# Gates split into parts already in the first batch, and p ahead of the next d in units 20 and 40

## The chip, the cores and the metric

The kernel runs on one core of a Trainium2 chip. The metric is the time of one execution on the device in microseconds (us). Before the change the median of three runs is 284.43 us.

## The reference

Two blocks follow one another. First an attention with sketched features: for each of 4 batches and 4 heads, with 1088 positions and head dimension 32,

```python
def phi(x):
    a = np.einsum('rd,bhsd->bhsr', S1, x)
    b = np.einsum('rd,bhsd->bhsr', S2, x)
    return np.einsum('bhsi,bhsj->bhsij', a, b).reshape(*x.shape[:-1], r * r)
q_p, k_p = (phi(q), phi(k))
kv = np.einsum('bhsf,bhsd->bhfd', k_p, v)
z = np.sum(k_p, axis=2)
num = np.einsum('bhsf,bhfd->bhsd', q_p, kv)
den = np.einsum('bhsf,bhf->bhs', q_p, z)[..., None] + 1e-06
attn = num / den
```

with r = 8. Its output becomes x, 4352 tokens by 128 channels. Then a gated feed-forward block with 1536 hidden channels: `g = x @ w_gate`, `val = x @ w_val`, `out = (g * sigmoid(g) * val) @ w_out`. The inputs q, k and v are float32; the sketches and weights come as float64 and are narrowed in the kernel.

## The kernel before, in words

The tokens stand on the free axis: `xT` holds x transposed, 128 channels by 4352 tokens. The hidden channels are 12 chunks of 128. A **unit** is one chunk for one block of tokens: a gate product and a value product on TensorE into PSUM, a Silu on ScalarE (`sg`), and their product on VectorE, written to a slot of `hbuf` or `late`. A **down product** multiplies such a slot by a chunk of `wo` and adds to the output block's PSUM bank; after 12 of them the block is turned and stored.

The instructions are put down in one order that is written out by hand, and each engine works through its own part of it. There are two stages.

*First batch* (tokens 0 to 1087, blocks 0 to 2 of 384, 384 and 320 tokens). `unit` (L1020) makes plain FP32 products. Six of its units are "late" ones: ScalarE copies the value product out, and GpSimd multiplies it by `sg` afterwards (`catch_up`, L1047); `doubles` (L964) finds room for these six `sg`. The other thirty units of the batch are emitted by the loop over `z`, 0 to 29; from z = 17 on each is followed by a down product and by a piece of the next batch's attention (`parts_of(1)`, which advances the generator `attentions`). The loop also splits the value weights `wv` (see below). After it, a `while todo` loop emits the remaining down products three at a time with the rest of the attention of batch 1: the denominators and products of query features (`query_step`, L744, tiles `dot`, `den`, `phq`, `phT`) on VectorE, and at last `numerators` (L773), 64 small matmuls (L783) that are copied to `xT` (L800) half by ScalarE and half by VectorE.

*Later blocks* (`line`: blocks 3 to 9, six of 480 tokens and one of 384; 84 units numbered y = 0 to 83). Here products are split. A weight w is parted by `cut_weights` (L841) in four rows of steps: w1 = a shortened copy (ScalarE), low = w - w1 (VectorE for `wg`, GpSimd for `wv`), wb = low x 4096 (ScalarE), and wd = w1 - wb (one operation on VectorE or GpSimd). All are recorded as L872. Tokens are split likewise by `cut_tokens` (L874) into x1, x0 and xd. A split product is three passes in the faster FP32R type, added in PSUM: **d** is wd by xd (L985, in `start_unit`), which ScalarE then scales in place in PSUM (L989); **p** is w1 by x1 and wb by x0 (L1004 and L1005, in `finish_unit`), added on top of the scaled d. Silu (L1007) and the product (L1012) follow.

`start_unit(y + 1)` is emitted ahead of `finish_unit(y)`, so that the scaling of one unit lies beside the passes of the one before. A unit takes a pair of PSUM banks from `pair()`, which chooses among three pairs the one used longest ago. Down products come after `finish_unit(y)`, once more than five hidden chunks are waiting; in units 0 to 4 there is none. At y in `GROUPS` (4, 6, 20, 22, 40) a group of small matmuls of the attention of the coming batches is put in front; at 20 and 40 it begins with `numerators`, which takes two pairs.

In units 0 to 19 only the value product is split: the gate product is a plain FP32 matmul (L999). The weights of the gates are split during units 0 to about 10, with `low` in `late`. From y = 20 (`GATES`) on both are split. The tile names show it: `w`, `wb`, `wd` are the parts of `wv`, and `graw`, `gphq` those of `wg`. Some chunks of blocks 6 to 8 have split down products, too; they aren't touched.

Of the kernel before, what the change touches and what calls it, by code (L numbers as in the profile page):

```python
# [7 lines left out]
FP32 = mybir.dt.float32  # L8
# [4 lines left out]
AF = mybir.ActivationFunctionType  # L13
# [6 lines left out]
def kernel(  # L20
# [28 lines left out]
    nc = tc.nc  # L49
    P = nc.NUM_PARTITIONS  # L50
# [18 lines left out]
    BW = 64 * XS  # L69
# [33 lines left out]
    def hold(*tags):  # L103
        for t in tags:
            held.update((place[t], place[t] + 1) if t in "ab" else (place[t],))
# [761 lines left out]
    def take(steps, n):  # L867

        for _ in range(n):
            if steps:  # L870
                f, args = steps.pop(0)
                f(**args)  # L872
# [86 lines left out]
            out=hd, in0=whole(h0), scalar=-BETA, in1=whole(h1), op0=ALU.mult, op1=ALU.add  # L959
        ))  # L960

    room = [None, 2]

    def doubles(k):  # L964

        if room[1] + k > 2:
            room[:] = fpool.tile([P, 2, WB], FP32, tag="sgl", name="sum", bufs=4), 0
        at = room[1]
        room[1] += k
        return room[0][:, at : at + k, :]  # L970

    WHOLE = 1.0 + 1.0 / BETA
    sums_of = {}

    def start_unit(y, both=False):

        i, j = line[y // NCH], y % NCH
        n = blocks[i][1]  # L980
        xd = x_parts[i][2][:, 0:n]
        ws = (wg, wv) if both else (wv,)
        ps = sums_of[y] = pair(y)[:, :, 0:n]
        for w in ws:
            nc.tensor.matmul(  # L985
                ps[:, w is wv], w_parts[id(w), j // 3][2][:, j % 3, :], xd, start=True, stop=True
            )
        d = ps if both else ps[:, 1]
        nc.scalar.activation(d, d, AF.Copy, scale=-1.0 / BETA / WHOLE)  # L989

    def finish_unit(y, both=False):
        i, j = line[y // NCH], y % NCH
        t0, n = blocks[i]
        x1, x0, _ = (x[:, 0:n] for x in x_parts[i])
        ps = sums_of.pop(y)
        now(before, y)
        for w in (wg, wv):
            if w is wg and not both:
                nc.tensor.matmul(  # L999
                    ps[:, 0], wg[:, j, :], xT[:, t0 : t0 + n], start=True, stop=True  # L1000
                )
                continue
            w1, wb = (w_parts[id(w), j // 3][k][:, j % 3, :] for k in range(2))
            nc.tensor.matmul(ps[:, w is wv], w1, x1, start=False, stop=False, skip_group_check=True)  # L1004
            nc.tensor.matmul(ps[:, w is wv], wb, x0, start=False, stop=True, skip_group_check=True)  # L1005
        sg = fpool.tile([P, WB], FP32, tag="sg", name="sg", bufs=5)[:, 0:n]
        nc.scalar.activation(sg, ps[:, 0], AF.Silu, scale=WHOLE if both else 1.0)  # L1007
        slot_of[i, j] = slots.pop(0)
        hj = slot_of[i, j]
        hidden[i, j] = hj  # L1010
        todo.append((i, j))
        nc.vector.scalar_tensor_tensor(  # L1012
            out=hj[:, 0:n], in0=ps[:, 1], scalar=WHOLE, in1=sg, op0=ALU.mult, op1=ALU.mult
        )
        let_go(y)
        now(behind, y)
        if (i, j) in DOWN:
            cut_hidden(y, i, j)

    def unit(i, j, late=False, between=(None, None)):  # L1020


        t0, n = blocks[i]
        g, u = bank(), bank()
        for o, w in ((g, wg), (u, wv)):
            if between[0] and w is wv:
                between[0]()
            nc.tensor.matmul(  # L1028
                o[:, 0:n], w[:, j, :], xT[:, t0 : t0 + n], start=True, stop=True
            )  # L1030
        sg = doubles(1)[:, 0, :] if late else fpool.tile([P, WB], FP32, tag="sg", name="sg", bufs=5)
        nc.scalar.activation(sg[:, 0:n], g[:, 0:n], AF.Silu)  # L1032
        slot_of[i, j] = slots.pop(0)
        hj = slot_of[i, j]
        hidden[i, j] = hj
        todo.append((i, j))
        if late:
            if between[1]:
                between[1]()
            nc.scalar.copy(hj[:, 0:n], u[:, 0:n])  # L1040
            lates.append((hj[:, 0:n], sg[:, 0:n]))
        else:
            nc.vector.tensor_tensor(  # L1043
                out=hj[:, 0:n], in0=sg[:, 0:n], in1=u[:, 0:n], op=ALU.mult
            )

    def catch_up():  # L1047
        o, sg = lates.pop(0)
        nc.gpsimd.tensor_tensor(out=o, in0=o, in1=sg, op=ALU.mult)


    def down(y=None):

        i, j = todo.pop(0)
        n = SPLIT if i == LAST else blocks[i][1]
        if j == 0:
            acc[i] = bank("g1" if i == 1 else "g2" if i in line[2::2] else "acc")
        mine = [c for c in range(NCH) if (i, c) in DOWN]
        if mine and j == mine[0]:
            acc[i, "p"] = bank("acc" if i in line[2::2] else "g2")  # L1060
        sides = dict(start=(j == 0), stop=(j == NCH - 1))
        if j in mine:
            w1, wb, wd = [down_parts[x][:, FINE.index(j), :] for x in ("w1", "wb", "wd")]
            h1, h0, hd = h_parts.pop((i, j))
            nc.tensor.matmul(acc[i][:, 0:n], wd, hd, **sides)  # L1065
            p = acc[i, "p"][:, 0:n]
            nc.tensor.matmul(p, w1, h1, start=(j == mine[0]), stop=False)  # L1067
            nc.tensor.matmul(p, wb, h0, start=False, stop=(j == mine[-1]))  # L1068
            if j == mine[-1]:
                copy_out(y, i, n)  # L1070
        else:
            w = down_parts["scaled"][:, PLAIN.index(j), :] if mine else wo[:, j, :]
            nc.tensor.matmul(acc[i][:, 0:n], w, hidden[i, j][:, 0:n], **sides)  # L1073
        if i != LAST:
            hidden.pop((i, j))
            slots.append(slot_of[i, j])
        if j == NCH - 1:
            if mine:
                put_together(y, i, n)
            else:  # L1080
                store(i, n)
# [209 lines left out]
    for z, (i, j) in enumerate(seq):  # L1291
        if z == 17:
            free_banks.pop()
            turn[0] %= 4
        unit(i, j)
        for p in parts.get(z, ()):
            part(*p)
        if z in (24, 25, 26):
            catch_up()
        if z == 6:  # L1300
            load_k(1)
            load_v(1, [nc.sync] * 4)
            load_q(1)
        if z >= 17:
            todo.remove(order[0])
            todo.insert(0, order.pop(0))
            down()
        if z == 20:
            lows = [
                pool.tile([P, 3, P], FP32, tag=tag, name="low", bufs=bufs)[:]  # L1310
                for pool, tag, bufs in ((apool, "qb", 2), (apool, "dT", 2), (apool, "rd", 2), (apool, "qb", 2))
            ]
            first, low, second, third = cut_weights(wv, lows, nc.gpsimd)
        if z in (20, 21):
            take(first, 2)
        if z == 21:
            take(low, 3)
        if z == 25:
            take(second, 3)
        if z >= 17:  # L1320
            parts_of(1)
        if z == 26:
            take(low, 1)
            take(third, 3)
        if z == 29:
            take(second, 1)
            take(third, 1)
    todo.sort()
    x_steps = None
    while todo:  # L1330
        for _ in range(min(3, len(todo))):
            down()
        if begun[0] and not x_steps:
            x_steps = cut_tokens(HEAD, nc.vector)
            run(x_steps)
        parts_of(1 + (begun[0] and len(todo) > 2))
# [7 lines left out]


    END = len(line) * NCH
    GROUPS, GATES = (4, 6, 20, 22, 40), 20

    token_steps = {}
    for m, i in enumerate(line[1:], 1):  # L1350
# [2 lines left out]
            token_steps.setdefault(at, []).append(gen)  # L1353
    oldest[0] = True
    hold("acc")
    lows = [late[:, c, :].rearrange("p (c f) -> p c f", f=P) for c in range(4)]
    gate_rows = []
    down_steps = cut_down()
    start_unit(0)
    for y in range(END):  # L1360
        if y in GROUPS:
            group()
        if y == GATES:
            hold("g2")
        if y + 1 < END:
            start_unit(y + 1, y + 1 >= GATES)
        finish_unit(y, y >= GATES)
        for _ in range(2):

            if len(todo) > min(5 + (todo[0] == (line[1], 0)), END - y + 1):  # L1370
                down(y)
        parts_of(y < GATES or y % 2 == 0)
        if y == 0:
            gate_rows = cut_weights(wg, lows, nc.vector)
        for n, row in enumerate(gate_rows):
            if y >= (0, 2, 6, 6)[n]:
                take(row, 1)
        for gen in token_steps.get(y, ()):
            next(gen, None)
        if y in range(24, 38, 2):  # L1380
            next(down_steps, None)
# [43 lines left out]
```

## Time and profile before

| | us |
|---|---|
| median of 3 runs | 284.43 (284.11 to 284.86) |
| the profiled execution's own time | 284.74 |
| its span, first to last instruction | 283.0 |
| TensorE busy | 275.2 |
| ScalarE busy | 175.2 |
| VectorE busy | 174.1 |
| GpSimd busy | 75.3 |

The profile is of one execution. PE is TensorE, DVE VectorE, ACT ScalarE, POOL GpSimd; L12 is line 12 of the kernel. A row of the timeline gives the start, the busy time, the engine, the line and the operation, the tile that is written and the one that is read, and how many instructions it holds; in brackets the idle time before it and what ended it. TensorE works on several matmuls at a time, so starts and durations of neighbouring rows overlap; the period from one row to the next of its kind is the measure. An FP32 matmul is recorded as two. The granted clock of TensorE was 0.997.

The first batch's last numerators are at about 87 us, unit 0 begins at 93 us, unit 20 lies near 142 us, unit 40 near 189 us.

### The profile page before, as it was taken

How to read it: one execution, taken by the hardware profiler on the slowest of the kernel's cores; microseconds unless marked ns; L12 is line 12 of the kernel's file. 1: busy time of each engine (PE TensorE's matmuls, PEld its weight loads, DVE VectorE, ACT ScalarE, POOL GpSimd, SP SyncE). 2: the span in 40 equal slices, each digit the busy share in tenths (PEclk: the TensorE clock that was granted, in tenths of full speed). 3: DMA queues.
4: the chain of work that ended last, by engine and by line, in shares of the span. 5: the costliest groups of instructions: out<-in, count | busy, mean ns of one | idle time of the engine just before them, and what ended most of it. 6: DMA issues, size and time to landing. Idle time of an engine off the chain costs nothing.

```text
span 283.0 us, 5508 instructions
## 1 busy us (share of the span) xinstructions
PE 275.2 (97%) x2134; PEld 192.3 (68%) x2134; DVE 174.1 (62%) x327; ACT 175.2 (62%) x323; POOL 75.3 (27%) x93
## 2 busy tenths in 40 slices
PE   7899999999999999999999999989999999999994
PEld 6645565666656676555577767757777777778993
DVE  3997987976395985987544575435436444644531
ACT  2468566633401856645367776858788888887750
POOL 3314432279510720250010140013314233231000
PEclk9999999999999999999999999999999999999998
DMA  6573195222231123000100020002000200100101
GB/s 191 162 225 94 43 270 167 81 79 81 68 56 28 27 89 86 2 0 10 26 18 0 0 36 2 0 2 35 0 1 0 37 0 0 27 10 1 20 15 31
DMA packets 26139, 14.30 MB, mean 51 GB/s; under 512 B 19840, under 2 KB 24192, under 8 KB 26112
## 3 DMA queue, kind: packets, MB, share of 16 engines
q1 hardware_dynamic: 25456, 13.84, 19.1%
q8 instruction: 17, 0.28, 0.4%
q10 hardware_dynamic: 656, 0.10, 0.2%
q14 instruction: 10, 0.08, 0.1%
HBM read 11.41 MB, written 2.23 MB: 48 GB/s over the span
## 4 chain that ended last, share of the span: by engine, by line
PE 94%; DVE 2%; DMA 2%; ACT 1%; issue 0%; SPq 0%
PE PS L1073 26%; PE PS L1028 15%; PE PS L985 11%; PE PS L1005 11%; PE PS L1004 11%; PE PS L999 6%; PE PS L783 2%; PE PS L357 2%; PE PS L345 2%; DMA kld<-in_k_dram 2%; PE PS L391 2%; PE PS L1068 1%; PE PS L1065 1%; PE PS L1067 1%; PE PS L1101 1%; PE PS L500 1%
## 5 line engine op out<-in xcount | busy, mean ns | idle before, releaser
L1012 DVE SCALAR_TENSOR_TENSOR hbuf<-PS,sg 128x480 f32<-128x480 f32 (+1 forms) x84 | 54.0, 642 | 74.6 <-ACT sg L1007 73.3
L989 ACT ACTIVATE PS<-PS 128x960 f32<-128x960 f32 (+2 forms) x84 | 70.3, 838 | 39.3 <-PE PS L985 38.7
L1073 PE MATMUL PS<-hbuf,wo 128*128 128x480 f32 (+3 forms) x142 | 57.5, 505 | 0.0
L1007 ACT ACTIVATE sg<-PS 128x480 f32<-128x480 f32 (+1 forms) x84 | 46.7, 556 | 4.6 <-PE PS L999 3.7
L985 PE MATMUL PS<-xd,gphq 128*128 128x480 f32 (+1 forms) x64 | 40.3, 630 | 0.8 <-ACT xT L800 0.8
L1004 PE MATMUL PS<-x,w 128*128 128x480 f32 (+1 forms) x84 | 38.7, 461 | 0.0
L985 PE MATMUL PS<-xd,wd 128*128 128x480 f32 (+1 forms) x84 | 35.8, 428 | 0.0
L1073 PEld LDWEIGHTS PS<-hbuf,wo 128*128 128x128 f32 x142 | 26.6, 189 | 8.2 <-issue 0.9
L1005 PE MATMUL PS<-x,wb 128*128 128x480 f32 (+1 forms) x84 | 31.5, 375 | 0.0
L1028 PE MATMUL PS<-xT,wg 128*128 128x384 f32 (+1 forms) x72 | 28.7, 480 | 0.0
L1028 PE MATMUL PS<-xT,wv 128*128 128x384 f32 (+1 forms) x72 | 28.0, 471 | 0.2 <-DVE wv L289 0.2
L1032 ACT ACTIVATE sg<-PS 128x384 f32<-128x384 f32 (+1 forms) x30 | 13.9, 466 | 21.3 <-PE PS L1028 19.6
L985 PEld LDWEIGHTS PS<-xd,wd 128*128 128x128 f32 x84 | 15.9, 189 | 12.3 <-issue 9.0
L1004 PE MATMUL PS<-x,graw 128*128 128x480 f32 (+1 forms) x64 | 23.9, 374 | 0.0
L1005 PE MATMUL PS<-x,graw 128*128 128x480 f32 (+1 forms) x64 | 23.7, 370 | 0.0
L1073 PE MATMUL PS<-hbuf,scaled 128*128 128x480 f32 x42 | 20.3, 564 | 0.0
L1004 PEld LDWEIGHTS PS<-x,w 128*128 128x128 f32 x84 | 15.8, 188 | 6.0 <-issue 3.8
L1005 PEld LDWEIGHTS PS<-x,wb 128*128 128x128 f32 x84 | 15.8, 188 | 5.5 <-issue 4.0
L1028 PEld LDWEIGHTS PS<-xT,wv 128*128 128x128 f32 x72 | 13.4, 190 | 8.9 <-DVE hbuf L1043 0.9
L985 PEld LDWEIGHTS PS<-xd,gphq 128*128 128x128 f32 x64 | 12.0, 188 | 10.9 <-ACT PS L989 7.5
L999 PE MATMUL PS<-xT,wg 128*128 128x480 f32 x40 | 19.3, 564 | 0.0
L1028 PEld LDWEIGHTS PS<-xT,wg 128*128 128x128 f32 x72 | 12.9, 189 | 9.3 <-issue 1.2
(171 smaller groups left out, 415.0 us busy)
## 6 DMA issues: line engine op xcount, KB each, us to landing
kld<-in_k_dram SPq DMA_DIRECT2D x4, 544.0 KB, 4.5
vld<-in_v_dram SPq DMA_DIRECT2D x12, 144.0 KB, 5.2
qld<-in_q_dram SPq DMA_DIRECT2D x3, 544.0 KB, 3.4
raw<-in_moe_w_out_dram SPq DMA_DIRECT2D x4, 384.0 KB, 4.7
raw<-in_moe_w_gate_dram SPq DMA_DIRECT2D x3, 384.0 KB, 3.6
raw<-in_moe_w_val_dram SPq DMA_DIRECT2D x3, 384.0 KB, 3.3
out_dram<-o SPq DMA_DIRECT2D x16, 60.0 KB, 1.9
vld<-in_v_dram SPq DMA_DIRECT2D x4, 112.0 KB, 4.3
```

The lines of the kernel that those rows point to most:

```text
L345: nc.tensor.matmul(ps[32 * a : 32 * a + 32, 96 * (c - c0) : 96 * (c - c0) + 96], qT[:, 4 * c + a, :], s123[:, a : a + H, :, :].rearrange(" ...
L357: nc.tensor.matmul(ps[32 * a : 32 * a + 64, 64 * (c - c0) : 64 * (c - c0) + 64], kT[:, c, a : a + 2, :].rearrange("p a t -> p (a t)"), s12 ...
L985: nc.tensor.matmul(ps[:, w is wv], w_parts[id(w), j // 3][2][:, j % 3, :], xd, start=True, stop=True)
L989: nc.scalar.activation(d, d, AF.Copy, scale=-1.0 / BETA / WHOLE)
L999: nc.tensor.matmul(ps[:, 0], wg[:, j, :], xT[:, t0 : t0 + n], start=True, stop=True)
L1004: nc.tensor.matmul(ps[:, w is wv], w1, x1, start=False, stop=False, skip_group_check=True)
L1005: nc.tensor.matmul(ps[:, w is wv], wb, x0, start=False, stop=True, skip_group_check=True)
L1007: nc.scalar.activation(sg, ps[:, 0], AF.Silu, scale=WHOLE if both else 1.0)
L1012: nc.vector.scalar_tensor_tensor(out=hj[:, 0:n], in0=ps[:, 1], scalar=WHOLE, in1=sg, op0=ALU.mult, op1=ALU.mult)
L1028: nc.tensor.matmul(o[:, 0:n], w[:, j, :], xT[:, t0 : t0 + n], start=True, stop=True)
L1032: nc.scalar.activation(sg[:, 0:n], g[:, 0:n], AF.Silu)
L1073: nc.tensor.matmul(acc[i][:, 0:n], w, hidden[i, j][:, 0:n], **sides)
```

## The change

The splitting of the gate weights moves from the later blocks into the first batch: copies w1 at z = 23 and 24, the four subtractions at z = 25 to 28 on VectorE, copies wb at z = 27 and 28, and the four last combinations in the `while todo` loop, two at a time, once fewer than nine down products are left. `low` and the six late `sg` share one tile, `room`, in the place of `doubles`. With the parts there from the start, `start_unit` and `finish_unit` lose their argument `both`: all units have three-pass gate products, and the scaling covers both banks of the pair in all of them. In units 20 and 40 `finish_unit(y)` is put down ahead of `start_unit(y + 1)`. `hold("g2")` at y = 20 goes.

```diff
-    room = [None, 2]
-    def doubles(k):
-...
+    room = const.tile([P, 10, BW], FP32, tag="room", name="room", bufs=1)
...
-    def start_unit(y, both=False):
+    def start_unit(y):
...
-        ws = (wg, wv) if both else (wv,)
         ps = sums_of[y] = pair(y)[:, :, 0:n]
-        for w in ws:
+        for k, w in enumerate((wg, wv)):
             nc.tensor.matmul(
-                ps[:, w is wv], w_parts[id(w), j // 3][2][:, j % 3, :], xd, start=True, stop=True
+                ps[:, k], w_parts[id(w), j // 3][2][:, j % 3, :], xd, start=True, stop=True
             )
-        d = ps if both else ps[:, 1]
-        nc.scalar.activation(d, d, AF.Copy, scale=-1.0 / BETA / WHOLE)
+        nc.scalar.activation(ps, ps, AF.Copy, scale=-1.0 / BETA / WHOLE)
-    def finish_unit(y, both=False):
+    def finish_unit(y):
...
-        for w in (wg, wv):
-            if w is wg and not both:
-                nc.tensor.matmul(
-                    ps[:, 0], wg[:, j, :], xT[:, t0 : t0 + n], start=True, stop=True
-                )
-                continue
-            w1, wb = (w_parts[id(w), j // 3][k][:, j % 3, :] for k in range(2))
-            nc.tensor.matmul(ps[:, w is wv], w1, x1, start=False, stop=False, skip_group_check=True)
-            nc.tensor.matmul(ps[:, w is wv], wb, x0, start=False, stop=True, skip_group_check=True)
+        for k, w in enumerate((wg, wv)):
+            w1, wb = (w_parts[id(w), j // 3][t][:, j % 3, :] for t in range(2))
+            nc.tensor.matmul(ps[:, k], w1, x1, start=False, stop=False, skip_group_check=True)
+            nc.tensor.matmul(ps[:, k], wb, x0, start=False, stop=True, skip_group_check=True)
...
-        nc.scalar.activation(sg, ps[:, 0], AF.Silu, scale=WHOLE if both else 1.0)
+        nc.scalar.activation(sg, ps[:, 0], AF.Silu, scale=WHOLE)
...
-        sg = doubles(1)[:, 0, :] if late else fpool.tile([P, WB], FP32, tag="sg", name="sg", bufs=5)
+        sg = room[:, len(lates) + caught[0], :] if late else fpool.tile([P, WB], FP32, tag="sg", name="sg", bufs=5)
...
+        if z == 23:
+            lows = [room[:, 6 + c, :].rearrange("p (c f) -> p c f", f=P) for c in range(4)]
+            gates = cut_weights(wg, lows, nc.vector)
+        for row, at in enumerate(((23, 24), (25, 26, 27, 28), (27, 28))):
+            if z in at:
+                take(gates[row], 4 // len(at))
     todo.sort()
...
         for _ in range(min(3, len(todo))):
             down()
+        if len(todo) < 9:
+            take(gates[3], 2)
...
-    GROUPS, GATES = (4, 6, 20, 22, 40), 20
+    GROUPS, WIDE, EASY = (4, 6, 20, 22, 40), (20, 40), 20
...
-    lows = [late[:, c, :].rearrange("p (c f) -> p c f", f=P) for c in range(4)]
-    gate_rows = []
...
-        if y == GATES:
-            hold("g2")
+        if y in WIDE:
+            finish_unit(y)
         if y + 1 < END:
-            start_unit(y + 1, y + 1 >= GATES)
-        finish_unit(y, y >= GATES)
+            start_unit(y + 1)
+        if y not in WIDE:
+            finish_unit(y)
...
-        parts_of(y < GATES or y % 2 == 0)
-        if y == 0:
-            gate_rows = cut_weights(wg, lows, nc.vector)
-        for n, row in enumerate(gate_rows):
-            if y >= (0, 2, 6, 6)[n]:
-                take(row, 1)
+        parts_of(y < EASY or y % 2 == 0)
```

More of the change, by code (lines that the diff above doesn't have):

```diff
@@ L960, in cut_hidden @@
         ))
-    room = [None, 2]
-    def doubles(k):
[L966 to L970, printed above, removed]
+    room = const.tile([P, 10, BW], FP32, tag="room", name="room", bufs=1)
     WHOLE = 1.0 + 1.0 / BETA
     sums_of = {}
-    def start_unit(y, both=False):
+    def start_unit(y):
         i, j = line[y // NCH], y % NCH
@@ L981, in start_unit @@
         xd = x_parts[i][2][:, 0:n]
-        ws = (wg, wv) if both else (wv,)
         ps = sums_of[y] = pair(y)[:, :, 0:n]
-        for w in ws:
+        for k, w in enumerate((wg, wv)):
             nc.tensor.matmul(
-                ps[:, w is wv], w_parts[id(w), j // 3][2][:, j % 3, :], xd, start=True, stop=True
+                ps[:, k], w_parts[id(w), j // 3][2][:, j % 3, :], xd, start=True, stop=True
             )
-        d = ps if both else ps[:, 1]
-        nc.scalar.activation(d, d, AF.Copy, scale=-1.0 / BETA / WHOLE)
-    def finish_unit(y, both=False):
+        nc.scalar.activation(ps, ps, AF.Copy, scale=-1.0 / BETA / WHOLE)
+    def finish_unit(y):
         i, j = line[y // NCH], y % NCH
-        t0, n = blocks[i]
+        n = blocks[i][1]
         x1, x0, _ = (x[:, 0:n] for x in x_parts[i])
@@ L1045, in unit @@
             )
+    caught = [0]
     def catch_up():
         o, sg = lates.pop(0)
+        caught[0] += 1
         nc.gpsimd.tensor_tensor(out=o, in0=o, in1=sg, op=ALU.mult)
```

## The prediction

> **What bounds the kernel now.** First the table of engines: TensorE is busy for nearly the whole span, and no other engine comes near.
>
> ```profile
> PE 275.2 (97%) x2134; PEld 192.3 (68%) x2134; DVE 174.1 (62%) x327; ACT 175.2 (62%) x323; POOL 75.3 (27%) x93
> ```
>
> So the time is TensorE work plus the few places where TensorE stands still. Next TensorE's timeline (start, busy time, line): two neighbouring down products (L1073) in the units 0 to 19, then two in the later units.
>
> ```profile
> 119.96 0.97 PE L1073 MATMUL PS<-hbuf,wo 128*128 128x480 f32 x2
> ...
> 122.22 0.97 PE L1073 MATMUL PS<-hbuf,wo 128*128 128x480 f32 x2
> ...
> 177.22 0.97 PE L1073 MATMUL PS<-hbuf,wo 128*128 128x480 f32 x2
> ...
> 179.34 0.97 PE L1073 MATMUL PS<-hbuf,wo 128*128 128x480 f32 x2
> ```
>
> A unit with a whole FP32 gate lasts 2.26 us (122.22 - 119.96), one with a split gate 2.12 (179.34 - 177.22). Nine units from 110.91 to 131.32 give 2.27 each. Third, the chain that ended last, where the units begin (first fence) and at unit 40 (second). It gives each matmul its share of the stream.
>
> ```profile
> 87.00 1.48 PE PS L783 x38
> 88.47 4.52 PE PS L1073 x16
> 93.00 0.44 PE PS L985 x2
> 93.44 0.81 PE PS L999 x2
> 94.24 0.21 PE PS L1004
> ```
>
> ```profile
> 186.63 2.06 PE PS L783 x39
> ...
> 188.71 0.71 ACT xT L800 x2
> ...
> 189.46 0.70 PE PS L985 x2
> 190.16 0.22 PE PS L1004
> ```
>
> An FP32 gate (L999) takes 0.81 us, one split pass 0.217 (0.21 to 0.22). Unit 0 follows the first batch's products without a gap. At unit 40 TensorE waits for ScalarE's copy of the numerators: two d passes end at 190.16, and would have ended at 188.69 + 0.43 = 189.12. That stop costs 1.04 us, 0.27 of it the restart. Last, ScalarE's and VectorE's timelines in the tail of the first batch, where the new work goes.
>
> ```profile
> 74.94 0.44 ACT L1032 ACTIVATE sg<-PS 128x320 f32<-128x320 f32 x1 [0.29 <-PE PS L1028]
> 75.27 0.70 ACT L593 COPY kab<-PS 128x320 f32<-128x320 f32 x2
> 76.66 0.44 ACT L1032 ACTIVATE sg<-PS 128x320 f32<-128x320 f32 x1 [0.69 <-PE PS L1028]
> ```
>
> ```profile
> 78.14 0.76 DVE L755 TENSOR_TENSOR qab<-qab,den 128x288 f32<-128x288 f32 x1
> 78.82 0.47 DVE L1043 TENSOR_TENSOR late<-sg,PS 128x320 f32<-128x320 f32 x1
> 79.22 0.94 DVE L380 TENSOR_TENSOR phq<-qab 128x768 f32<-128x768 f32 x1
> ...
> 84.64 0.98 DVE L765 STREAM_TRANSPOSE phT<-phq 128x768 f32<-128x768 f32 x1
> ```
>
> VectorE's chain ends at 85.62 with the last phT, which the numerators (L783, at 87.00) read: slack 1.38 us.
>
> **What the skill says.** The Trainium skill, "FP8 and Floating Point Precision", TensorE Precision Notes: a true FP32 product makes four passes. The trace has 0.81 / 0.217 = 3.7. "PSUM — Partial Sum Buffer", Engine vs sequencer instructions: the queues of ScalarE and VectorE are strict first in, first out, and matmuls start and end in program order. The rows above agree, so an instruction that waits holds all behind it. "ScalarE: Activation LUTs", Rules for kernel authors: about 0.3 us plus 0.83 ns an element. The scaling in PSUM (L989) takes 0.955 us for 960 elements and 0.56 for 480: the slope agrees, the fixed part here is 0.16 us. Durations of the trace are used.
>
> **The change, part by part.**
>
> *1. Gate products in units 0 to 19.* Removed: 20 FP32 matmuls of 0.81 us. Added: 20 x 3 passes of 0.217 = 0.651 us. That is 0.16 a unit, and 2.27 - 2.12 = 0.15 by the timelines. I take 20 x 0.15 = **-3.0 us**, all on TensorE's path.
>
> *2. The wider scaling and unit 0.* L989 now scales both halves: 0.955 us instead of 0.56 in these units. ScalarE needs 0.87 (start to start) + 0.45 for the Silu = 1.32 us a unit. Units with a down product last 2.12, and there p(y) comes 0.87 + 0.81 + 0.43 = 2.11 us after d(y) ends (four passes of p(y-1), a down product, d(y+1)), while the scaling needs 0.04 + 0.955 + 0.04: hidden, with 1.07 to spare. Unit 0 has no such cover. Before, the FP32 gate needed no scaled sum and hid the scaling. Now, counted from d(0)'s start: d(0) ends at 0.43, scaling from 0.47 to 1.42, p(0) starts at 1.46, and d(1) ended at 0.87. With the restart of 0.27 seen at unit 40 the bubble is 0.59 + 0.27 = **+0.85**. Units 1 to 3 have no down product either: TensorE 6 x 0.217 = 1.30 against ScalarE's 1.32. Following the first-in-first-out order: Silu(0) 2.22 to 2.79, product 0 2.84 to 3.50, d(3) (which takes its PSUM pair) 3.89. Scaling 2 ends at 4.01, p(2) starts at 4.32. Product 1 ends at 5.20, and d(4)'s value pass, which takes its bank, starts at 5.41. Nothing more waits, but the margins are 0.2 to 0.4. If all were missed, 3 x 0.3 = 0.9 more.
>
> *3. The splits in the first batch.* Eight ScalarE copies at z = 23, 24, 27, 28, four VectorE subtractions at z = 25 to 28, four combinations in the tail. They fall away in units 0 to 10, where they were hidden. A 128x384 split copy takes 0.41 start to start, a subtraction 0.55, a combination 0.53 (rows of L872). At z = 23 to 26 both engines are idle between units by more than they get (ScalarE waits 1.44 to 1.50 us per unit for TensorE). At z = 27 two copies come between the query copies (end 74.65) and Silu 28, which moves from 74.94 to about 75.42, and with it product 28 (75.49 to 75.97). The down product that takes its bank starts at 76.94: still hidden. At z = 28 the fourth copy waits for the fourth subtraction, which stands on VectorE behind the whole denominator chain up to L755. That chain moves by about 0.34, so L755 starts at 78.48 and gives way at 79.16; subtraction to 79.71, copy 79.80 to 80.31, then Silu 29, queued behind it, 80.21 to 80.65, then product 29 at 80.75 instead of 78.82. Behind that on VectorE stand the three phq and phT pairs: phT ends at 85.62 + 1.93 = 87.55. The numerators start at about 87.65 to 87.75 instead of 87.00: **+0.7**. Bounds: 0 if the copy finds its operand earlier, 1.3 if the ping-pong costs 0.3 at each of two hand-overs. Late next: the copy to xT, two combinations, x0 and xd end near 92.3. d(0) is due near 93.7, eight down products after the numerators (4.5 us), so these are covered; without the cover they would cost their 2 x 0.53. The key features and transposes after them run until about 96.0, before product 0 (93.7 + 2.84). The last wv copy waits behind Silu 29, and GpSimd's subtraction behind that copy is first needed by unit 9.
>
> *4. p in front of d in units 20 and 40.* At unit 40 p(40) (0.87 us) runs from 188.69 to 189.56 while ScalarE copies until 189.42, so d(41) finds its bank free. Gain 1.04, less up to 0.1: **-0.95**. Scaling 41 starts 0.04 after d(41), behind Silu 40, and ends near 191.0; p(41) comes after a down product and d(42), at 191.2. At unit 20 there is no stop before (the key products lie between), and p(21) comes 1.24 us after d(21), against 1.03 needed: 0, bounds 0 and +0.2.
>
> *5. Nothing.* The `room` tile holds the same six late gates. Fewer, fixed places change no wait, since no place is reused by a late gate. hold("g2") kept a bank that pair() never takes. No DMA is added or moved.
>
> Sum: -3.0 + 0.85 + 0.7 - 0.95 = -2.4 us. The profiled execution (284.74, of which 283.0 span and 1.74 around it) would become 282.3, span 280.6. It lies 0.3 above the median, so against 284.43 the forecast is **282.0**.
>
> **Rivals.** *B: the tail is hidden.* The slack of 1.38 us, or earlier VectorE starts, swallow part 3. For it: the chain moves by only 0.55 more than the slack. Against: two crossings between the engines. -3.1, 281.3. With most of unit 0's bubble covered too, 280.6. *C: more of it waits.* Units 1 to 3 run at the pace of ScalarE and the PSUM pairs (+0.9), or d(41) finds another wait (+0.9). For it: margins of 0.1 to 0.4. Against: the order worked out above. -1.5, or -0.6 with both: 282.9 to 283.8. *D: slower.* Each of the units 5 to 19 waits for its scaling, as unit 0 does. At 0.16 us a unit the gain of 2.4 is gone, at 0.25 the kernel is 1.3 us slower: 285.8. It decides once ScalarE reaches d's sum 1.07 us late in every unit. Against: units 21 to 39 have this same pattern with the wide scaling and run at 2.12.
>
> **How the numbers follow.** A (as summed, 281.4 to 282.6) 0.54, B 0.20, C 0.19, D 0.07. A measurement can tell about 0.3%, 0.85 us. A and B, and two thirds of C, are faster by more: 0.87. The rest of C and a little of D are within 0.3%: 0.07. Slower 0.06. The range takes in the two ends of B and most of C: 280.6 to 283.5.
>
> **What would show it.** Unit period 2.12 from unit 6 on, no FP32 gate products left in the units; in unit 0 a wait of p for the scaling of about 0.6 us; numerators of the first batch idle 0.6 to 0.8 on VectorE's phT, with Silu 29 near 80.2; no idle before d(41). The forecast is wrong if units 1 to 3 wait as unit 0 does, if the numerators come on time or over 1.3 us late, or if unit 40 still stops.

## The result and the profile after

The changed kernel takes 281.42 us (median of 4 runs, 281.24 to 282.09), the kernel before 284.56 beside it (4 runs). The ratio is 0.9895, 95% interval 0.9873 to 0.9917: 3.1 us faster. The profiled execution took 281.56 us (before 284.74), its span is 279.9 (before 283.0), and TensorE's granted clock was 1.0. The forecast had 282.0: right sign, inside the range, 0.6 us above the measured time.

First the table of engines of the changed kernel:

```profile
PE 273.3 (98%) x2154; PEld 195.5 (70%) x2154; DVE 174.3 (62%) x327; ACT 181.5 (65%) x323; POOL 76.9 (27%) x93
```

TensorE is still the bound. It lost 1.9 us of busy time. ScalarE gained 6.3, since the scaling is wider in 20 units. TensorE's timeline, two neighbouring down products among the units that had whole gates before:

```profile
119.34 0.97 PE L1062 MATMUL PS<-hbuf,wo 128*128 128x480 f32 x2
121.46 0.97 PE L1062 MATMUL PS<-hbuf,wo 128*128 128x480 f32 x2
```

A unit now lasts 2.12 us. (The lines have moved: d is L977, the scaling L980, p L990 and L991, Silu L993, the down product L1062.) The chain of waits around unit 0 of the changed kernel (start, us, what):

```profile
86.95 1.48 PE PS L783 x38
...
92.95 0.44 PE PS L977 x2
...
93.42 0.96 ACT PS L980
...
94.43 0.49 PE PS L990
```

The numerators (L783) come at 86.95 and are not late. In unit 0 TensorE has only d(1) to do beside the scaling and then stands until the scaling is through. p(0) ends its first two passes at 94.43 + 0.49 + 0.22 = 95.14. In an unbroken stream, with two passes of d(1) and two of p(0) right behind d(0), they would end at 93.40 + 0.86 = 94.26, which is 0.88 sooner. Then the same view at unit 20, and at unit 40:

```profile
137.18 2.04 PE PS L783 x39
...
143.24 0.36 PE PS L990
...
185.05 2.02 PE PS L783 x39
187.07 0.43 PE PS L990
...
189.40 0.42 PE PS L977 x2
189.82 0.36 PE PS L990
```

At unit 40 p stands right behind the numerators, and the stop of 0.71 us for ScalarE's copy is gone. New are two things. p(21) and p(41), the rows of 0.36, wait 0.14 for their scaling (a pass is 0.22). And the numerators of unit 20 take 2.04 us; in the kernel before the chain of waits has them with 1.66:

```profile
139.30 1.66 PE PS L783 x38
```

The chains of the two profiles, cut at marks that both have, give a ledger. It is TensorE's time and the rest after it; "predicted" is the prediction's sum, laid on the same marks. (d(4) now has two passes ahead of its mark, one more than before: 0.22 more in the second row and 0.22 less in the fourth.)

| stretch, from mark to mark | before | after | measured | predicted |
|---|---|---|---|---|
| start to the first numerators | 87.00 | 86.95 | -0.05 | +0.7 |
| to the end of unit 3 | 12.04 | 12.63 | +0.59 | +0.47 |
| units 4 and 5 (to the group at y = 6) | 6.50 | 6.21 | -0.29 | -0.30 |
| units 6 to 19 (to the numerators at y = 20) | 33.76 | 31.39 | -2.37 | -2.32 |
| numerators at y = 20 to the group at y = 22 | 7.35 | 7.88 | +0.53 | 0 |
| y = 22 to the numerators at y = 40 | 39.98 | 39.99 | 0 | 0 |
| numerators at y = 40 to d(42) | 5.20 | 4.35 | -0.85 | -0.95 |
| d(42) to VectorE's last copy (p(41) is in it) | 87.06 | 87.20 | +0.14 | 0 |
| last copy to the end of the span | 4.1 | 3.3 | -0.8 | 0 |
| sum | 283.0 | 279.9 | -3.1 | -2.4 |

TensorE's part is -2.3, where -2.4 was forecast: nearly the sum, but by luck. A term of +0.7 did not come, and +0.53 and +0.14 came that no term had. The 0.8 at the end is in no term. The granted clock, 0.997 and 1.0, explains none of this: the 40 us from y = 22 to y = 40 took the same in both. The first row can't carry much either, since the time up to the first numerators lies anywhere from 86.4 to 87.3 us in the traces of kernels that don't wait there. The last copy, from VectorE's timeline, of the changed kernel and then of the kernel before:

```profile
276.60 0.29 DVE L1379 COPY o_last<-PS 128x128 f32<-128x128 f32 x1 [1.34 <-PE PS L1090]
```

```profile
278.89 0.29 DVE L1388 COPY o_last<-PS 128x128 f32<-128x128 f32 x1 [1.33 <-PE PS L1101]
```

Until here the gain is 2.29 us; the same four stores follow in both.

### The profile page after: what moved, and what is told of

Same layout as the page of the kernel before. It is cut to its first block, busy times and chain, and to the rows that moved or that the text cites. A ratio compares the mean times of both kernels' runs of the same rounds, so it can differ in the third digit from the quotient of the medians.

```text
span 279.9 us, 5561 instructions
## 1 busy us (share of the span) xinstructions
PE 273.3 (98%) x2154; PEld 195.5 (70%) x2154; DVE 174.3 (62%) x327; ACT 181.5 (65%) x323; POOL 76.9 (27%) x93
## 4 chain that ended last, share of the span: by engine, by line
PE 94%; DVE 2%; DMA 2%; ACT 1%; issue 0%; SPq 0%
PE PS L1062 26%; PE PS L1014 16%; PE PS L990 13%; PE PS L977 13%; PE PS L991 13%; PE PS L783 2%; PE PS L357 2%; PE PS L345 2%; PE PS L391 2%; DMA kld<-in_k_dram 2%; PE PS L1057 1%; PE PS L1054 1%; PE PS L1056 1%; PE PS L1090 1%; PE PS L500 1%; PE PS L448 1%
## 5 line engine op out<-in xcount | busy, mean ns | idle before, releaser
L980 ACT ACTIVATE PS<-PS 128x960 f32<-128x960 f32 (+1 forms) x84 | 78.3, 934 | 37.1 <-PE PS L977 36.6
L1062 PE MATMUL PS<-hbuf,wo 128*128 128x480 f32 (+3 forms) x142 | 57.5, 505 | 0.0
L977 PE MATMUL PS<-xd,gphq 128*128 128x480 f32 (+1 forms) x84 | 52.2, 622 | 0.0
L993 ACT ACTIVATE sg<-PS 128x480 f32<-128x480 f32 (+1 forms) x84 | 46.6, 555 | 2.0 <-PE PS L991 1.3
L990 PE MATMUL PS<-x,graw 128*128 128x480 f32 (+1 forms) x84 | 32.1, 382 | 0.6 <-ACT PS L980 0.6
L1062 PEld LDWEIGHTS PS<-hbuf,wo 128*128 128x128 f32 x142 | 26.6, 189 | 8.2 <-issue 0.9
L991 PE MATMUL PS<-x,wb 128*128 128x480 f32 (+1 forms) x84 | 31.6, 376 | 0.0
L977 PE MATMUL PS<-xd,wd 128*128 128x480 f32 (+1 forms) x84 | 31.4, 374 | 0.0
L990 PE MATMUL PS<-x,w 128*128 128x480 f32 (+1 forms) x84 | 31.4, 374 | 0.0
L991 PE MATMUL PS<-x,graw 128*128 128x480 f32 (+1 forms) x84 | 31.3, 372 | 0.0
L977 PEld LDWEIGHTS PS<-xd,gphq 128*128 128x128 f32 x84 | 15.8, 188 | 12.5 <-ACT PS L980 9.6
L977 PEld LDWEIGHTS PS<-xd,wd 128*128 128x128 f32 x84 | 15.9, 189 | 12.2 <-issue 9.0
L1062 PE MATMUL PS<-hbuf,scaled 128*128 128x480 f32 x42 | 20.3, 564 | 0.0
L883 POOL TENSOR_TENSOR x<-xT,x 128x480 fp32r<-128x480 f32 (+1 forms) x6 | 7.1, 1178 | 42.8 <-ACT x L882 42.8
L990 PEld LDWEIGHTS PS<-x,graw 128*128 128x128 f32 x84 | 15.7, 187 | 4.3 <-ACT PS L980 1.6
L990 PEld LDWEIGHTS PS<-x,w 128*128 128x128 f32 x84 | 15.8, 188 | 2.1
```

The lines of the kernel that those rows point to most:

```text
L883: engine.tensor_tensor(out=x0[:, 0:n], in0=x, in1=whole(x1[:, 0:n]), op=ALU.subtract)
L977: nc.tensor.matmul(ps[:, k], w_parts[id(w), j // 3][2][:, j % 3, :], xd, start=True, stop=True)
L980: nc.scalar.activation(ps, ps, AF.Copy, scale=-1.0 / BETA / WHOLE)
L990: nc.tensor.matmul(ps[:, k], w1, x1, start=False, stop=False, skip_group_check=True)
L991: nc.tensor.matmul(ps[:, k], wb, x0, start=False, stop=True, skip_group_check=True)
L993: nc.scalar.activation(sg, ps[:, 0], AF.Silu, scale=WHOLE)
```

## The experiments

Times are medians, against which the kernel before had 284.42, 284.62 and 284.49 in the three groups. In the traces I compare the stretch from the first numerators to the last copy: 191.89 us before, 189.65 after the change.

**One part alone, and without it.** The changed kernel with d ahead of p again in units 20 and 40 (`no_wide`), and the kernel before with only that move (`only_wide`).

```diff
-    GROUPS, WIDE, EASY = (4, 6, 20, 22, 40), (20, 40), 20
+    GROUPS, WIDE, EASY = (4, 6, 20, 22, 40), (), 20
```

> The change without p in front of d (the order of units 20 and 40 as before). My theory: in the changed kernel's trace unit 40 gains 0.86 us (TensorE is 1.58 us ahead of the kernel before at the numerators and 2.44 ahead after p(40), d(41) and a down product), and gives 0.14 back where p(41) waits for the scaling; unit 20 gives 0.14 back for nothing. Without it the time is 0.86 - 0.14 - 0.14 = 0.6 us above the changed kernel: about 282.0. The stop of 1.04 us before d(41) is back. Rival (the three-pass gates alone remove that stop, the order is of no account): the same time as the changed kernel, 281.4.

> The kernel before with p in front of d in units 20 and 40 alone. My theory: 0.6 to 0.7 us faster than before, about 283.9; TensorE's end comes 0.6 to 0.9 earlier. Rival (the last 0.8 us of the changed kernel's gain, after TensorE's last matmul, belong to the change in itself): no part of that here, the stretch after the last matmul stays at 4.1 us; if that stretch only scatters from run to run, it can be 3.3 here too.

`no_wide` took 282.0 us (281.94 to 282.1), ratio 0.9909 (0.9894 to 0.9924). That is the expected time. Its chain of waits has the old stop at unit 40:

```profile
186.97 0.71 ACT xT L800 x2
...
187.72 0.70 PE PS L977 x2
```

`only_wide` took 283.26 (282.93 to 284.54), ratio 0.9967 (0.9955 to 0.9979): more than the 0.6 to 0.7 expected. TensorE's stretch is 191.36, 0.53 less than before: -0.69 at unit 40 and +0.16 at p(21). The rest is not TensorE's: the stretch after the last copy is 3.2 us instead of 4.1. So the move is worth 0.5 to 0.6 by both runs, and the end of the kernel changes with an edit that isn't near it.

**The tail of the first batch.** Either the fourth copy wb gets out of Silu 29's way (`tail_free`), or the fourth subtraction comes later, behind three unused ones of 128x384 (`tail_late`).

```diff
# tail_free
-        for row, at in enumerate(((23, 24), (25, 26, 27, 28), (27, 28))):
+        for row, at in enumerate(((23, 24), (25, 26, 27, 28), (27, 29))):
# tail_late, ahead of the subtraction at z = 28
+            for c in range(3):
+                nc.vector.tensor_tensor(out=lows_room[c], in0=wg[:, 9:12, :],
+                                        in1=wg[:, 6:9, :], op=ALU.subtract)
```

> The change, but the second pair of wb copies (z = 28) stands behind Silu 29 (z = 29), so that no copy waits for the fourth subtraction ahead of Silu 29. My theory: Silu 29 starts at about 76.7 instead of 79.67, VectorE's last phT ends near 86.0 instead of 86.58 (the subtraction itself stays in its chain), and the time doesn't move (281.4), since in the changed kernel the numerators start at 86.95 by TensorE's own queue. GpSimd's last wd subtraction comes back to about 77.6, beside L755: if L755's 0.76 us before against 0.46 after came from that neighbour, it is 0.76 again. Rival (the numerators of the changed kernel do wait for phT): faster by up to 0.5.

> The change with three more subtractions of 128x384 on VectorE (unused results) ahead of the fourth one at z = 28. Each takes 0.47 us start to start, 1.4 in all; phT ends near 88.0. My theory: the slack of the changed kernel at the numerators is 0.37 us (86.95 - 86.58), so 1.0 us of it reach TensorE, with a restart 1.0 to 1.3: about 282.5 to 282.7. Rival B as it was put (enough slack at that place to hide such a delay): 281.4.

First the changed kernel's own tail, ScalarE's timeline and then VectorE's:

```profile
79.24 0.52 ACT L872 ACTIVATE graw<-room 128x384 fp32r<-128x384 f32 x1 [2.46 <-DVE room L872]
79.67 0.42 ACT L1018 ACTIVATE sg<-PS 128x320 f32<-128x320 f32 x1
```

```profile
78.28 0.46 DVE L755 TENSOR_TENSOR qab<-qab,den 128x288 f32<-128x288 f32 x1
78.65 0.55 DVE L872 TENSOR_TENSOR room<-wg,graw 128x384 f32<-128x384 f32 x1
80.12 0.49 DVE L1029 TENSOR_TENSOR late<-sg,PS 128x320 f32<-128x320 f32 x1 [0.92 <-ACT sg L1018]
...
81.58 0.98 DVE L765 STREAM_TRANSPOSE phT<-phq 128x768 f32<-128x768 f32 x1
...
85.60 0.98 DVE L765 STREAM_TRANSPOSE phT<-phq 128x768 f32<-128x768 f32 x1
```

The predicted crossing is there: the copy waits 2.46 us for the subtraction, Silu 29 stands behind it, and product 29 starts 1.30 us later than before. But phT ends at 86.58 and not at 87.55, 0.37 before the numerators start. `tail_free` took 281.61 (281.41 to 281.75), ratio 0.9894 (0.9879 to 0.9909): no different from the changed kernel beyond the scatter, so the crossing costs nothing. `tail_late` took 282.58 (282.48 to 282.7), ratio 0.9929 (0.9914 to 0.9944), 1.2 us slower than the changed kernel, and here the numerators do wait, as TensorE's timeline shows:

```profile
87.80 1.57 PE L783 MATMUL PS<-phT,spread 32*32 32x288 f32 x64 [1.08 <-DVE phT L765]
```

The wait that was feared exists, and the changed kernel stands 0.4 us in front of it. In `tail_free` Silu 29 is early (76.81), and yet phT ends at 86.50, not at the 86.0 expected. VectorE's timeline of that kernel, then GpSimd's, tell why; the third row is GpSimd's in the kernel before:

```profile
77.83 0.93 DVE L753 TENSOR_SCALAR den<-den 128x36 f32<-128x36 f32 x1
```

```profile
77.73 1.00 POOL L872 TENSOR_TENSOR wd<-w,wb 128x384 fp32r<-128x384 f32 x1 [2.21 <-ACT wb L872]
```

```profile
77.59 1.00 POOL L872 TENSOR_TENSOR wd<-w,wb 128x384 fp32r<-128x384 f32 x1 [3.04 <-ACT wb L872]
```

L753 takes 0.18 in the changed kernel. Here it ends as GpSimd's operation does. In the kernel before it was L755 that started beside GpSimd's operation (77.59 to 78.59) and took 0.76 instead of 0.46. The Trainium skill, "SBUF — State Buffer", Who interferes with whom, says that VectorE and GpSimd share a pair of ports as an exclusive lock: an operation of VectorE with two inputs in SBUF, or a tensor_scalar in its two-port mode, and an operation of GpSimd that reads SBUF shut each other out until the first is done. These rows agree, 0.30 us in the one and 0.75 in the other. The reciprocal L754, which has one input, also started beside GpSimd's operation in the kernel before (77.72), and took the same 0.38 as in the changed kernel.

**Unit 0's bubble.** Either d(0) goes two down products ahead in the first batch (`cover0`), or unit 0 keeps its whole FP32 gate and scales only the value half (`gate0_whole`).

```diff
# cover0
         for _ in range(min(3, len(todo))):
+            if x_steps and len(todo) == 2:
+                start_unit(0)
             down()
...
-    start_unit(0)
# gate0_whole, in start_unit (in finish_unit the gate is then one FP32 matmul)
+            if y == 0 and k == 0:
+                continue
```

> The change, with unit 0's d (start_unit(0)) put down ahead of the last two down products of the first batch, so that its scaling lies beside 1.08 us of down products. My theory: p(0) finds the scaled sum ready, the bubble of 0.88 us in unit 0 goes, nothing else waits: 0.85 to 0.9 us below the changed kernel, about 280.6. Rival (units 1 to 3 run at ScalarE's pace anyway, 1.32 us and its hand-overs against 1.30): the bubble moves into units 1 to 3, and less than half of it is gained: 281.0 to 281.4.

> The change, but unit 0 has a whole FP32 gate product (0.81 us) as in the kernel before, and only its value sum is scaled. My theory: the FP32 gate covers the scaling as before; 0.88 of bubble go and 0.16 of gate time come back: about 0.7 us below the changed kernel, 280.7. Rival (unit 0's wait isn't for the wide scaling): no gain, 281.4 to 281.6.

`cover0` took 280.8 us (280.46 to 281.1), ratio 0.9832 (0.9799 to 0.9866); `gate0_whole` 280.77 (280.53 to 281.26), ratio 0.9834 (0.98 to 0.9868). TensorE's stretches are 188.93 and 188.92: each gives back 0.72 to 0.73 of the 0.88. For `gate0_whole` that is what was expected. `cover0` was expected to give all of it; its chain of waits has no row of ScalarE left, and d(3) takes 0.59 for its two passes, 0.16 more than the 0.43 of the others:

```profile
92.24 1.08 PE PS L1062 x4
93.31 0.43 PE PS L977 x2
93.74 0.22 PE PS L990
...
95.97 0.59 PE PS L977 x2
```

So the bubble goes, and a small part of it comes back in units 1 to 3, as the rival said of most of it.

**Silu 19 behind the scaling of d(20).** Why do the numerators at y = 20 take 0.38 more? They use two pairs of PSUM banks, the second of which is free when product 19 has read it. In the changed kernel's timeline of ScalarE, Silu 19 stands behind the scaling of d(20):

```profile
135.55 0.95 ACT L980 ACTIVATE PS<-PS 128x960 f32<-128x960 f32 x1 [1.45 <-PE PS L977]
136.42 0.56 ACT L993 ACTIVATE sg<-PS 128x480 f32<-128x480 f32 x1
```

Behind it comes VectorE's product 19, in the changed kernel and then in the kernel before:

```profile
137.02 0.66 DVE L998 SCALAR_TENSOR_TENSOR hbuf<-PS,sg 128x480 f32<-128x480 f32 x1 [1.25 <-ACT sg L993]
```

```profile
138.75 0.66 DVE L1012 SCALAR_TENSOR_TENSOR hbuf<-PS,sg 128x480 f32<-128x480 f32 x1 [1.80 <-ACT sg L1007]
```

In the changed kernel it ends at 137.68, when the numerators have begun (137.18), and the view of waits for 135 to 142 us has the weight load of the numerators waiting 0.5 us for this product. In the kernel before the scaling of d(20) was as wide already, and Silu 19 behind it, but unit 19's p had the FP32 gate and was 0.81 - 2 x 0.217 = 0.38 longer: product 19 ended at 139.41, 0.11 after the numerators' start (139.30). Now it ends 0.50 after it. The shorter p of unit 19 only brings TensorE to the same wait sooner. The order of unit 20 has no part in it: the numerators take 2.02 in `no_wide`, and 1.66 in `only_wide`. `wide4` puts p first in units 19 and 39 too, so that Silu comes ahead of the scaling.

```diff
-    GROUPS, WIDE, EASY = (4, 6, 20, 22, 40), (20, 40), 20
+    GROUPS, WIDE, EASY = (4, 6, 20, 22, 40), (19, 20, 39, 40), 20
```

> The change, with p ahead of the next d in units 19 and 39 too. In the changed kernel the numerators of units 20 and 40 take 2.04 and 2.02 us, against 1.66 at unit 20 before: they wait some 0.4 us for product 19 (or 39), whose Silu stands behind the scaling of unit 20 (40) on ScalarE. My theory: with Silu 19 and 39 ahead of that scaling the wait goes, both numerators take about 1.66: 0.75 us below the changed kernel, about 280.7. Rival (the numerators wait for something else, phT or the spread rows): they stay at 2.0, 281.4.

It took 280.29 us (280.26 to 280.38), ratio 0.9816 (0.9777 to 0.9855), with a stretch of 188.58, 1.07 less than the change. Its chain of waits at unit 20:

```profile
136.98 1.48 PE PS L783 x38
```

At unit 40 it is 1.48 too, from 2.02: 0.56 and 0.54 less, 1.10 together. That is more than the 0.75 expected, which took the 1.66 of the kernel before for a row without a wait. The kernel before had part of this wait at unit 20 (1.66) and all of it at unit 40 (2.06).

**Does scaling everywhere cost what it was feared to?** Rival D: each unit waits for its scaling. `act_extra` adds an unused ScalarE operation of 1024 elements in units 7 to 18 of the changed kernel; `gates10` keeps whole gates in units 0 to 9.

```diff
# act_extra, after the down products of unit y
+        if 7 <= y < 19:
+            nc.scalar.activation(late[:, 0:3, :].rearrange("p c w -> p (c w)")[:, 0:1024],
+                wg[:, 0:8, :].rearrange("p c f -> p (c f)"), AF.Copy, scale=CUT)
```

> The change with one more ScalarE copy of 1024 elements (about 0.9 us start to start, unused result) in each of the units 7 to 18. ScalarE's sum per unit becomes 1.32 + 0.9 = 2.2 us against TensorE's 2.115. My theory: the cover of about 0.8 us per unit is just used up and ScalarE sets the pace by some 0.1 us a unit: 12 x 0.1 = 1.2, with the first units' slack 0.5 to 1.3 above the changed kernel, 281.9 to 282.7. Rival D as it was put (each unit's p waits for the scaling already): nearly all of the 0.9 reaches TensorE in each unit, 12 x 0.9 = 10.8, 292.

> The change, but units 0 to 9 have whole FP32 gates (their parts are made in the first batch all the same), units 10 on three-pass gates. My theory: 0.153 us a unit (2.268 before, 2.115 after, by the period of down products) times ten come back, 1.5, and unit 0's bubble of 0.88 and the later 0.16 of waits in units 3 to 6 go: TensorE's last matmul ends 0.4 to 0.5 us later than in the changed kernel, counted from the first numerators. Rival (the unit period was not the gain, the earlier splits were): no later at all. The ScalarE queue has 457 entries here against 468 in the changed kernel and 454 before, so the end of the span may be 3.3 or 4 us long (see the run on the fetch): 281.9 or 282.7.

`act_extra` took 283.71 us (283.28 to 285.25), ratio 0.9975 (0.9962 to 0.9987): 2.3 above the changed kernel, more than my theory gave. ScalarE's timeline in two rounds of it:

```profile
131.91 1.10 ACT L1369 ACTIVATE late<-wg 128x1024 f32<-128x1024 f32 x1
132.85 1.02 ACT L980 ACTIVATE PS<-PS 128x960 f32<-128x960 f32 x1
...
134.19 1.11 ACT L1369 ACTIVATE late<-wg 128x1024 f32<-128x1024 f32 x1
```

ScalarE is then full with 0.94 + 0.89 + 0.45 = 2.28 us a unit. TensorE does not feel it at once. Its chain of waits, by the starts of down products, and then in units 17 and 18:

```profile
119.35 0.81 PE PS L1062 x2
...
121.47 0.81 PE PS L1062 x2
...
128.19 0.81 PE PS L1062 x2
...
130.49 0.81 PE PS L1062 x2
...
134.36 0.94 ACT late L1369
135.30 0.86 ACT PS L980
136.16 0.49 ACT sg L993
```

For the first seven rounds with the added operation the period stays at 2.12 while ScalarE falls behind; then three rounds take 2.29. That makes 0.6 us. Then come units 17 and 18 with no down product between them, where TensorE's own work is only 1.30 us, and the chain runs through ScalarE up to the numerators at y = 20. Against the changed kernel these come 2.70 us late, counted from the first numerators, and then take 1.49 instead of 2.04, so that 2.15 are left. The mechanism is the expected one (ScalarE sets the pace once it is full), but the expected 0.1 us a unit left out the units without a down product, and so came out too small. In the changed kernel itself ScalarE needs 1.34 of 2.12, and no unit from 6 to 19 waits for its scaling. `gates10` took 281.93 (281.6 to 282.05), ratio 0.9901 (0.9872 to 0.993), with a stretch of 190.23. By `gate0_whole` a whole gate in unit 0 is worth -0.73, and nine more whole gates put 9 x 0.15 = 1.35 back, together +0.62. Measured +0.58.

**The end of the kernel.** The stretch after the last copy was 4.1 us in the kernel before and 3.2 to 3.3 in the changed kernel and in all its variants. `before_again` is the kernel before, unchanged. `fetch_shift` is the kernel before with 14 one-element copies on ScalarE, one in each of the units 24 to 37; the built program's ScalarE stream has 454 entries before, 468 after the change (14 more waits), and 468 in `fetch_shift`; the traces, with two fewer records each, have the same differences.

```diff
+        if 24 <= y < 38:
+            nc.scalar.copy(pad[:], rebias[:])
```

> The kernel before, unchanged, profiled a second time. In its first profile the span goes on for 4.1 us after the last VectorE copy starts (278.89 to 283.0), and 3.2 to 3.3 us in the five other kernels profiled so far; TensorE's own gain in the changed kernel is only 2.3 us of the 3.1 by the spans. If the long end belongs to the program, it is 4.1 here again and 0.8 us of the gain come from the end of the kernel, which the change does not name. If it scatters, it can be 3.3 here, and the median of the kernel before stays at 284.4.

> The kernel before with 14 one-element copies on ScalarE, one in each of the units 24 to 37, where ScalarE has time to spare. In the two profiles of the kernel before, the last packet of the instruction queue that serves ScalarE's stream comes 1 to 2 us after the last stores are issued, in the changed kernel 8 to 12 us ahead of it; the changed kernel has 14 more entries (waits) in ScalarE's queue. My theory: the late fetch lengthens the end of the kernel, and with 14 more entries it comes early: the stretch after the last VectorE copy is 3.3 us instead of 4, TensorE's own times don't change, and the time is 0.7 to 0.9 below the kernel before, 283.6 to 283.8. Rival (the long end has to do with what the kernel before computes or with when its stores fall): 284.4 to 284.6.

`before_again` took 284.58 us (283.98 to 286.07), ratio 0.9991 (0.9975 to 1.0007), and its last stretch was 3.9. `fetch_shift` took 283.47 (20 runs, 283.22 to 284.95; three of them at 283.95 or more), ratio 0.996 (0.9947 to 0.9973): 1.0 us faster than the kernel before by doing more. Its last copy starts at 278.38 and its span ends at 281.6, 3.2 later; the stop at unit 40 and the order of TensorE are as before, and TensorE's stretch, 191.68, is 0.2 shorter. The DMA view has two queues named "instruction"; one of them, q14, has ten packets of 8 KB spread over the span. Its row in the kernel before, for 279.0 to 281.0 us (the stores are issued from 279.21), and in `fetch_shift`, for 269.6 to 273.6 us (stores from about 278.7):

```profile
q14 instruction: 1, 0.01, 1.9%
```

```profile
q14 instruction: 1, 0.01, 0.8%
```

In the kernel before, a packet of this queue falls among the last stores, and they take 1.9 us to land. In `fetch_shift` and in the changed kernel the last packet comes some 9 us ahead of the stores, and they take 1.4 and 1.6. The more entries ScalarE's stream has, the earlier this packet is: near 280.6 with 454, 278.5 with 456 (`only_wide`), 276.9 with 457 (`gates10`), 269.7 with 468. In `only_wide` it comes just as the stores are issued (278.30), in `gates10` shortly before; both ended in 3.2 to 3.3 us. So the end was long only where the packet came 1 us and more after the issue (in the kernel before near 280.6, stores from 279.21). Shown is that 14 more copies on ScalarE, far from the end, shorten the end. That it is the number of entries and the packet's place, and that the changed kernel's waits do the same, is argued from these rows.

**Both cures.** `cover0_wide4` has the edits of `cover0` and of `wide4`.

> The change with both cures: unit 0's d ahead of the first batch's last two down products, and p ahead of d in units 19 and 39 too. In their own traces they took 0.72 and 1.07 us off TensorE's stretch from the first numerators to the last matmul. My theory: they lie at different places and add up: 1.8 us below the changed kernel, about 279.6. Rival (units 19 and 20 wait for what cover0 brings forward): 280.2.

It took 279.74 us (279.45 to 279.96), ratio 0.9825 (0.9796 to 0.9854), with a stretch of 187.86: 1.79 less than the change, as 0.72 + 1.07 = 1.79 say. It beats both kernels.

## Why the prediction was right and wrong

*Step 1, the gate products: right.* 0.15 a unit was forecast, and the ledger's rows for units 4 to 19 have -2.66 against -2.62.

*Step 2, the wide scaling: right for unit 0 and the rounds with a down product.* p(0)'s first two passes end 0.88 us later than they would in an unbroken stream (forecast 0.85), and two different cures give 0.72 back. Units 1 to 3 wait for almost nothing (0.08 at d(4)), as its first-in-first-out order said. That no unit from 6 to 19 waits for its scaling is shown by the period of 2.12 and by the row of -2.37 for -2.32. The 0.3 us that the prediction quotes from the Trainium skill, "ScalarE: Activation LUTs", Rules for kernel authors, is stated there for an activation whose bias is a pointer operand. The scaling is given no bias, so the 0.16 measured does not contradict it.

*Step 3, the tail: the crossing right, the term wrong.* "+0.7" measured as nothing. The numerators came on time, which the prediction itself had named as a sign that it is wrong. The copy does wait for the fourth subtraction, with Silu and product 29 behind it, but VectorE's phT ended at 86.58 and not at 87.55, and so inside the slack of 1.38. The shift of the chain was 0.96, not 1.93. Of the 0.97 between, 0.20 is the denominator chain, which moved by 0.14 and not by 0.34. 0.31 is L755, which no longer ran beside GpSimd's operation: that operation waits for a copy that the same crossing pushed back, and ran 3 us later (80.58 for 77.59). 0.12 is in the hand-overs between VectorE and ScalarE. The rest, about 0.35, is a gap of 0.47 ahead of the first phT transpose, which the kernel before and `only_wide` have, and the changed kernel, `no_wide` and `tail_free` don't; what makes it stays open. I moved the rows of before as blocks, stretched durations and gaps with them.

*Step 4, p ahead of d: right where it gains, incomplete in what it costs.* Unit 40 gave -0.85 for -0.95. The two scalings that come after (21 and 41) were said to be ready and were 0.14 late each; for unit 20 this is in the bounds of 0 to +0.2. What no bound held is +0.38 at the numerators of unit 20. It isn't caused by the move, since `no_wide` has it too and `only_wide` doesn't, and belongs to step 1: the 0.38 that unit 19's p saves is given back at once, because the numerators need the banks of product 19, and Silu 19 still stands behind the scaling of d(20). Step 2 followed that queue for units 0 to 3 only. It should have followed it to the place where a group takes two pairs at once. `wide4` shows the wait by removing it.

*Step 5, "nothing": wrong.* The end became 0.8 us shorter. By `fetch_shift` the likely cause is that extra waits on ScalarE are extra entries of its stream. No row of the kernel before's profile that I had read pointed to it.

Rival B has the nearest time (281.3) and half of the reason (the tail is hidden); the 0.8 at the end and the 0.7 at units 20, 21 and 41 about cancel, so that its exact time is luck. Of the forecast's own error, the 0.7 that failed and the 0.7 that was missed cancel, and the end is what is left. Rival D fell by the period of 2.12; with another 0.94 us of ScalarE work in twelve units they did come to wait, after seven rounds.

## What to carry to other kernels

When the bounding engine's work in a round gets shorter, look for the place where the next thing it does waits for another engine's first-in-first-out queue: there the saving may be given back (here at a group that takes two pairs of banks, 0.4 us), until that queue's order is changed too. A pipeline that hides a stage pays for it in its first round, and the cure is to start that round ahead of the last work before it (0.7 us here). When a sum of small terms comes near, lay it on marks of both traces before believing it: here a term of 0.7 that failed and waits of 0.7 that were missed cancelled, and 0.8 at the end was in no term.

## What the runs showed of the hardware that I had not expected

- Fourteen one-element copies on ScalarE, in the units 24 to 37, made the kernel 1.0 us faster (ratio 0.996, 0.9947 to 0.9973), 0.7 to 0.9 of it in the last stretch (3.2 us for 3.9 to 4.1).
- GpSimd's operation of 1.00 us stretched some VectorE operations that started beside it: a tensor_scalar of 128x36 from 0.18 to 0.93 us, to the end of GpSimd's own run, and a tensor_tensor of 128x288 from 0.46 to 0.76. A reciprocal of 128x36 stayed at 0.38. The other way round, in the changed kernel, GpSimd's operation started 0.05 us after a VectorE tensor_tensor of 128x768 (80.58 and 80.53) and took 1.76 instead of 1.00.
